# Other slots for kept keys and loads, and whole heads in one load, in a decode kernel over two caches

## The chip, the cores and the metric

The kernel runs on one core of one Trainium2 chip. The core has TensorE (PE, with its weight loads as PEld), VectorE (DVE), ScalarE (ACT), GpSimd (POOL) and SyncE (SP), which here issues every load, and 16 DMA engines that move the data. The metric is device time in microseconds, the median of the runs shown. Before the change it is 1115.87 us over three runs (1115.45 to 1117.47).

## The reference

Eight sequences of one token each (448 numbers) go through attention A, a mixing MLP B, then A and B again with the same weights and the same caches:

```python
x = A_x
x = x + _A_ref(_layernorm(x, axis=-1), A_k_cache, A_v_cache, A_wq, A_wo)
x = x + _B_ref(_layernorm(x, axis=-1), B_w1, B_w2, B_w3, B_w4)
x = x + _A_ref(_layernorm(x, axis=-1), A_k_cache, A_v_cache, A_wq, A_wo)
x = x + _B_ref(_layernorm(x, axis=-1), B_w1, B_w2, B_w3, B_w4)

def _A_ref(x, k_cache, v_cache, wq, wo):        # Hq, Dh = 16, 256; caches (8, 8, 4096, 256), bf16
    q = (x @ wq).reshape(B, Sq, Hq, Dh).transpose(0, 2, 1, 3)
    k = jnp.repeat(k_cache, 2, axis=1)
    v = jnp.repeat(v_cache, 2, axis=1)
    p = softmax(einsum("bhqd,bhkd->bhqk", q, k) * Dh ** -0.5)
    o = jnp.einsum("bhqk,bhkd->bhqd", p, v)
    return o.transpose(0, 2, 1, 3).reshape(B, Sq, Hq * Dh) @ wo
```

With one token, the shifts inside B leave zeros of its first part, so B comes down to `x + h2` with two layer norms and `w3`, `w4`. The key and value caches have 134 MB each; each of them is wanted twice.

## The kernel before

**Units and parts.** A unit is one key/value head of one sequence in one of the two attention passes: `(p, b, g)`, with pass p 1 or 2, sequence b, head g. The keys of a head are 2 MB, and so are the values. They are handled in four parts of 512 KB. A part lies in one slot: 4 KB on each of 128 partitions. The slab holds 31 slots of `UNIT` = 2048 bf16 elements a partition, side by side. In HBM partition p owns 16 KB of a head in one piece (32 rows of 256 numbers), of which part s is the s-th 4 KB.

**Keys.** A key part is loaded raw, transposed by DVE into another slot (L560, two instructions a part, in `transposes`), and the raw slot becomes free. PE multiplies the transposed part with the queries (L651, 16 matmuls, in `k_part`). For heads 2 to 7 the transposed keys stay in their slots from pass 1 to pass 2. Heads 0 and 1 are `loose`: their keys are loaded and transposed again for pass 2. Two parts of head 4 (`parked`) are kept in PSUM banks instead, and ScalarE copies them back into a slot when pass 2 comes near (L518).

**Values.** A value part is read by PE straight from its slot (L628, 16 matmuls, in `v_part`) and loaded again in pass 2. In all there are 320 key parts and 512 value parts.

**Order.** The order of units is written out: per sequence pass 1 of its heads, then two units of other sequences (`lone`) that lie beside the dense layers of the sequence (a generator, `mid_steps`), then pass 2. The unit that ends a pass 1 is in `ends`; `fence` holds the unit with which pass 2 of a sequence begins, because its queries must be done. Each unit has four steps q; at each step the key part of the unit and value parts of an earlier one are multiplied. After the key parts come the maximum over the scores (DVE L666, PE L674, DVE L684), the exponential (ACT L687), the way into rows (PE L700 and L710, ACT L718), the sum (DVE L725, POOL L729), and at the end the scaling of the output (ACT L597).

**Loads.** `loads` is a list in a fixed order, made from the step at which a part is due. `pump` is called wherever a slot comes free, takes loads off the list as long as more than `RESERVE` = 1 slot is free, and issues each on SP (L534). The first loads of weights are spliced in (L543). `free` is the list of slots; `under_way` counts parts that are issued and not yet used up. Stretches between a fence and the next end are `calm`; loads that fall due there are in `wide`, and those some units from its borders in `firm`. If a load of an even part has its neighbour near it in the list and in `wide`, both are loaded in one go into an even slot and the next one. If no such two are free, and `ENOUGH` = 7 parts are under way and the neighbour is in `firm`, `pump` returns and waits; else the part goes alone.

The program is written straight into each engine's queue: an instruction waits in its own queue until the slots that it reads and writes are ready, and what stands behind it waits too. Which slot is taken therefore decides on whom a load, a transpose or a copy waits.

Of the kernel before, what the change touches and what calls it, by code (L numbers as in the profile page):

```python
# [17 lines left out]
RESERVE = 1  # L18
# [4 lines left out]
LEAD = 1  # L23
LAG = 6
ENOUGH = 7
PAIR_VIEW = 12
SETTLE = 3
BEFORE = 1
# [3 lines left out]
def kernel(  # L32
# [333 lines left out]
    loose = heads[: G - KEEP]  # L366

    second = [2, 3, 6, 7, 4, 5]
    parked = {(second[-1], 4 - PARKED + i): i for i in range(PARKED)}
# [3 lines left out]
    lone = {b: [(1, b + 2, g) for g in loose] for b in range(4)}  # L373
    lone.update({4: [(1, 6, 0)], 5: [(1, 6, 1)], 6: [(1, 7, 1)], 7: [(2, 5, 1)]})
    units = []
# [29 lines left out]
    t = 0  # L405
    while t < n_units:
# [5 lines left out]
        n = 1  # L412
# [3 lines left out]
        for j in range(parts_):  # L416
            m = n // parts_ + (j < n % parts_)
# [26 lines left out]
    for t in order:  # L444
        for s in range(4):
            i = late_v.get((t, s), 4 * t + s + LAG)
            if t in ends or units[t + 1 : t + 2] == [GAP]:
                i = 4 * t + (6, 6, 7, 7)[s]
            elif t + 1 == n_units:
                i = 4 * t + (5, 5, 6, 7)[s]  # L450
# [3 lines left out]
    loads = []  # L454
    wide = set()
    calm = [any(f < t for f in [-1] + list(fence) if not any(f < e < t for e in ends)) for t in range(n_units + 2)]
    firm = set()
    at_ease = [all(calm[max(t - SETTLE, 0) : t + BEFORE]) for t in range(n_units + 1)]
    k = 0
    for i in range(4 * n_units + 8):  # L460
        n = len(loads)
# [8 lines left out]
        t, q = divmod(i + 2, 4)  # L470
# [3 lines left out]
    free = list(range(N_SLOTS))  # L474
    raw_of, v_of, kt_of = {}, {}, {}
    under_way = [0]

    def take():

        lone = [x for x in free if x ^ 1 not in free]  # L480
        x = min(lone or free)
        free.remove(x)
        return x

    def take_two():

        both = [x for x in free if x % 2 == 0 and x + 1 in free]
        if both:
            free.remove(both[0])
            free.remove(both[0] + 1)  # L490
        return both[:1]

    extra = []
    for c in range(3):
# [13 lines left out]
    def pump():  # L508
        while loads and len(free) > RESERVE:
            kind, t, i = loads[-1]  # L510
            _, b, g = units[t]
            if kind == "p":
                loads.pop()
                x = take()
                dst = slots[x].rearrange("p (e q c x) -> p q c e x", e=4, q=2, c=4)
                for j in range(2):
                    src = park[parked[g, i]][j][:].bitcast(BF16)
                    nc.scalar.copy(dst[:, j], src.rearrange("p (c e x) -> p c e x", c=4, e=4))  # L518
                kt_of[(1, b, g), i] = x
                continue  # L520
            cache, of = (A_k_cache, raw_of) if kind == "k" else (A_v_cache, v_of)
            n, two = 1, (kind, t, i + 1)
            if i % 2 == 0 and two in wide and two in loads[-PAIR_VIEW:]:
                x = take_two() if len(free) > RESERVE + 1 else []
                if x:
                    n, x = 2, x[0]
                    loads.remove(two)
                elif under_way[0] >= ENOUGH and two in firm:
                    return
            loads.pop()  # L530
            if n == 1:
                x = take()
            src = cache[b, g].rearrange("(p s e) d -> p s (e d)", s=4, e=8)
            nc.sync.dma_start(  # L534
                slab[:, UNIT * x : UNIT * (x + n)].rearrange("p (s d) -> p s d", s=n),
                src[:, i : i + n],
            )
            for m in range(n):
                of[t, i + m] = x + m
            under_way[0] += n  # L540
            n_loads[0] += n
            if n_loads[0] >= 8 and extra:
                nc.sync.dma_start(*extra.pop(0))  # L543
# [3 lines left out]
    def transposes(i):  # L547


        while len(parts) - len(todo) < by[i]:  # L550
            t, s = todo[-1]
            if 4 * t + s > i and ((t, s) not in raw_of or not free):
                return
            todo.pop()
            raw = raw_of.pop((t, s))
            kt = kt_of[units[t], s] = take()
            src = slots[raw].bitcast(FP32).rearrange("p (q c e i) -> p q c e i", q=2, c=4, e=4)
            dst = slots[kt].bitcast(FP32).rearrange("p (e q c r) -> p q c e r", e=4, q=2, c=4)
            for q in range(2):
                nc.vector.transpose(dst[:, q], src[:, q])  # L560
            _, b, g = units[t]
            if (g, s) in parked:
                for q in range(2):
                    dst = park[parked[g, s]][q][:].rearrange("p (c e r) -> p c e r", c=4, e=4)
                    nc.vector.transpose(dst, src[:, q])
            free.append(raw)
            under_way[0] -= 1
            pump()
# [49 lines left out]
    def v_part(t, s):  # L618
        if s == 0:
            at = PO + 4 * (nth[t] % n_po)  # L620
            pos[t] = pyb[:, at : at + 4].rearrange("p (k h) -> p k h", h=2)
            if nth[t] == n_po // 2:
                nc.vector.memset(pyb[:, PO : PO + 4 * (len(order) - n_po)], 0.0)
        v = v_of.pop((t, s))
        vv = slots[v].rearrange("p (c d) -> p c d", d=Dh)
        for c in range(8):
            for k in range(2):
                nc.tensor.matmul(  # L628
                    pos[t][:, k, :],
                    vv[:, c, 128 * k : 128 * k + 128],  # L630
                    pts[t][:, 8 * s + c, :],
                    start=(t == 0 and s == 0 and c == 0 and k == 0),
                    stop=True,
                    skip_group_check=True,
                )
        free.append(v)
        under_way[0] -= 1
        pump()

    def k_part(t, s):  # L640
        u = units[t]
        p, b, g = u
        if s == 0:
            assert t not in runs or t in ready
            scs[t] = scb[t % 2][:, 0:64].rearrange("p (c b h) -> p c b h", b=4, h=2)
        key = (u if fresh(u, s) else (1, b, g)), s
        ktv = slots[kt_of[key]].rearrange("p (e c m x) -> p e c m x", e=4, c=2, x=2)
        for c in range(2):
            for db in range(4):
                for x in range(2):  # L650
                    nc.tensor.matmul(  # L651
                        scs[t][:, 2 * s + c, :, :],
                        ktv[:, db, c, :, x],
                        Qblk[run_of[t][0]][:, run_of[t][1], db, x, :, :],
                        start=(db == 0 and x == 0),
                        stop=(db == 3 and x == 1),
                    )
        if p == 2 or g in loose or (g, s) in parked:
            free.append(kt_of.pop(key))
            pump()  # L660
# [129 lines left out]
    for t in range(n_units + 1):  # L790
        cur = t < n_units
        for q in range(4):
            i = 4 * t + q
            if cur:
                if t in fence and q == 0:
                    flush()
                    while (fence[t], 1) not in q_done:
                        next(dense[0])
                        flush()
                    flush()  # L800
                    make_blocks(t)
                late = q == 0 and t and not beside[t]
                if beside[t]:
                    transposes(i)
                flush()
                if not late and not beside[t]:
                    transposes(i)
                if units[t]:
                    k_part(t, q)
# [4 lines left out]
            if cur and late:  # L814
                transposes(i)
# [130 lines left out]
```

## Time and profile before

| | |
|---|---|
| median of three runs | 1115.87 us |
| the profiled execution | 1116.44 us |
| its span, first to last instruction | 1114.6 us |
| moved by DMA | 449.77 MB, mean 404 GB/s |
| PE, PEld busy | 686.8 us, 640.3 us |
| DVE, ACT, POOL busy | 550.7 us, 307.2 us, 104.4 us |
| loads of keys | 126 of 512 KB, 97 of 1024 KB |
| loads of values | 252 of 512 KB, 130 of 1024 KB |
| DVE transposes (L560) | 640, mean 687 ns |
| granted TensorE clock | 1.00 |

The page's slices cut the span into 40 equal parts; the figure for DMA is the share of time in which the 16 DMA engines were busy, in tenths. A row of the waits says which engine and line waited, for whom, how many microseconds in all, how often, and the longest. In a row of the windows stand the stretch, its length, busy time and instructions of PE, PEld, DVE, ACT and POOL, the clock, the DMA share and GB/s. In the timeline stand start, duration, engine, line, operation, operands, count, and in brackets the idle time before it with what ended it; rows of SPq are issues of loads. An engine that waits costs nothing as long as another is the bottleneck.

### The profile page before, as it was taken

What the parts mean: (1) busy time and instruction counts of PE and PEld (TensorE: products, weight loads), DVE (VectorE), ACT (ScalarE), POOL (GpSimd) and SP (SyncE); (2) the same over time, 40 slices, a digit from 0 to 9 for tenths busy, and PEclk for the clock granted to TensorE, in tenths of its full rate; (3) what the DMA queues carried; (4) which work ended last, traced back from release to release, by engine and by line L of the source; (5) the groups of instructions that cost most, each with busy time, mean ns of one, the idle gap of its engine ahead of it and who ended that gap; (6) DMA issues with size and microseconds to landing.
All of it is one profiled execution on the core that took longest, in us unless ns stands there. A gap on an engine that the chain in (4) does not pass through costs nothing.

```text
span 1114.6 us, 46349 instructions
## 1 busy us (share of the span) xinstructions
PE 686.8 (62%) x20737; PEld 640.3 (57%) x20737; DVE 550.7 (49%) x1305; ACT 307.2 (28%) x1360; POOL 104.4 (9%) x156
## 2 busy tenths in 40 slices
PE   3345675666756566565756667565757566655765
PEld 2334564665646566565656557555756566655765
DVE  4347554644446445554555535553447435554332
ACT  1112124321233212422233212422143212422231
POOL 0001001110011100110011000110011000100001
DMA  9999999999999999999999999999999999999992
GB/s 364 393 417 425 401 417 423 424 418 395 417 423 424 402 401 419 422 424 390 414 420 424 400 410 416 421 423 412 395 419 425 407 411 397 422 422 405 384 413 101
DMA packets 94503, 449.77 MB, mean 404 GB/s; under 512 B 9936, under 2 KB 15968, under 8 KB 64864
## 3 DMA queue, kind: packets, MB, share of 16 engines
q1 hardware_dynamic: 94304, 446.81, 98.4%
q8 instruction: 162, 2.65, 0.8%
q14 instruction: 37, 0.30, 0.1%
HBM read 446.77 MB, written 0.01 MB: 401 GB/s over the span
## 4 chain that ended last, share of the span: by engine, by line
DMA 39%; PE 15%; ACT 6%; issue 5%; DVE 5%; POOL 0%; SPq 0%; DVEq 0%; ACTq 0%; POOLq 0%
DMA slab<-in_A_v_cache_dram 31%; DMA slab<-in_A_k_cache_dram 8%; PE bank L628 5%; PE bank L651 3%; DVE slab L560 3%; ACT pt L718 2%; PE bank L137 2%; ACT slab L518 1%; ACT pe L687 1%; DVE small L684 1%; PE bank L674 1%; PE bank L710 1%; ACT pt_far L718 1%; PE bank L700 1%; PE bank L313 1%
## 5 line engine op out<-in xcount | busy, mean ns | idle before, releaser
L560 DVE STREAM_TRANSPOSE slab<-slab 128x512 f32<-128x512 f32 x640 | 414.7, 687 | 217.6 <-DMA slab<-in_A_k_cache_dram 173.2
L628 PEld LDWEIGHTS <-slab 128*128 128x128 bf16 x8192 | 273.3, 106 | 288.6 <-DMA slab<-in_A_v_cache_dram 223.7
L628 PE MATMUL bank<-pt,slab 128*128 128x2 bf16 x7168 | 261.0, 166 | 235.4 <-DMA slab<-in_A_v_cache_dram 163.6
L651 PE MATMUL bank<-Qblk,slab 128*128 128x8 bf16 x8192 | 297.0, 168 | 77.0 <-DVE slab L560 39.3
L651 PEld LDWEIGHTS <-slab 128*128 128x128 bf16 x8192 | 267.6, 105 | 88.1 <-DVE slab L560 46.4
L687 ACT ACTIVATE pe<-bank,small 128x32 bf16<-128x32 f32 x256 | 61.7, 297 | 407.6 <-DVE small L684 407.5
L729 POOL TENSOR_TENSOR small<-small 128x2 f32<-128x2 f32 x112 | 78.4, 700 | 774.1 <-DVE small L725 774.1
L718 ACT CAST pt<-bank 32x64 bf16<-32x64 f32 x448 | 91.1, 203 | 108.2 <-PE bank L710 104.2
L684 DVE TENSOR_REDUCE small<-bank 128x2 f32<-128x256 f32 x128 | 54.1, 422 | 104.9 <-PE bank L674 104.6
L725 DVE TENSOR_REDUCE small<-bank 128x2 f32<-128x64 f32 x128 | 27.2, 212 | 118.8 <-ACT pt L718 102.6
L166 ACT CAST Qblk<-bank 32x32 bf16<-32x32 f32 (+1 forms) x272 | 48.5, 178 | 109.4 <-PE bank L160 107.0
L674 PE MATMUL bank<-rows,small 128*128 128x128 bf16 x256 | 48.5, 293 | 10.9 <-DVE small L666 10.9
L666 DVE TENSOR_REDUCE small<-bank 128x2 bf16<-128x64 f32 x128 | 26.4, 206 | 55.4 <-PE bank L651 55.2
L628 PE MATMUL bank<-pt_far,slab 128*128 128x2 bf16 x1024 | 36.8, 166 | 26.2 <-DMA slab<-in_A_v_cache_dram 24.6
L710 PE MATMUL bank<-pe,rows 128*128 128x64 bf16 x512 | 51.0, 240 | 1.1 <-issue 1.1
L710 PEld LDWEIGHTS <-rows 128*128 128x128 bf16 x512 | 33.6, 123 | 28.2 <-issue 27.6
L700 PE MATMUL bank<-pe,small 128*128 128x64 bf16 x128 | 27.2, 212 | 31.8 <-ACT pe L687 29.9
L182 PEld LDWEIGHTS <-wo_sb 128*128 128x128 bf16 x1152 | 35.5, 104 | 9.9 <-issue 8.8
L182 PE MATMUL bank<-OT,wo_sb 128*128 128x1 bf16 x1024 | 33.3, 165 | 7.0 <-ACT OT L597 4.5
L137 PEld LDWEIGHTS <-wq_sb 128*128 128x128 bf16 x864 | 30.6, 106 | 12.0 <-issue 7.4
L518 ACT COPY slab<-park 128x1024 bf16<-128x1024 bf16 x32 | 30.1, 1028 | 8.8 <-DVE slab L560 8.7
L137 PE MATMUL bank<-small,wq_sb 128*128 128x1 bf16 x768 | 28.1, 165 | 6.0 <-issue 6.0
(113 smaller groups left out, 384.1 us busy)
## 6 DMA issues: line engine op xcount, KB each, us to landing
slab<-in_A_v_cache_dram SPq DMA_DIRECT2D x130, 1024.0 KB, 13.0
slab<-in_A_v_cache_dram SPq DMA_DIRECT2D x252, 512.0 KB, 8.1
slab<-in_A_k_cache_dram SPq DMA_DIRECT2D x97, 1024.0 KB, 13.7
slab<-in_A_k_cache_dram SPq DMA_DIRECT2D x126, 512.0 KB, 8.9
wo_sb<-in_A_wo_dram SPq DMA_DIRECT2D x4, 896.0 KB, 11.7
wq_sb<-in_A_wq_dram SPq DMA_DIRECT2D x3, 1024.0 KB, 6.9
w_sb<-in_B_w_dram SPq DMA_DIRECT2D x1, 1568.0 KB, 12.4
w_sb<-in_B_w_dram SPq DMA_DIRECT2D x3, 448.0 KB, 16.7
```

Source lines behind the costliest of these rows:

```text
L137: nc.tensor.matmul(pv[:, i, j, :], cols(big[:, c, :], m + i * half), rows[:, c, :], start=(i == 0 and j == 0 and c == 0), stop=True, skip_ ...
L166: nc.scalar.copy(dst, src)
L182: nc.tensor.matmul(y[:, c, :], chunk(wo_sb[:, k, :], c), o[:, k, :], start=False, stop=True, skip_group_check=True,)
L560: nc.vector.transpose(dst[:, q], src[:, q])
L628: nc.tensor.matmul(pos[t][:, k, :], vv[:, c, 128 * k : 128 * k + 128], pts[t][:, 8 * s + c, :], start=(t == 0 and s == 0 and c == 0 and k ...
L651: nc.tensor.matmul(scs[t][:, 2 * s + c, :, :], ktv[:, db, c, :, x], Qblk[run_of[t][0]][:, run_of[t][1], db, x, :, :], start=(db == 0 and x ...
L674: nc.tensor.matmul(mzs[t][:, 128 * h : 128 * h + 128], pm[:, h : h + 1].to_broadcast([128, 128]), ident, start=True, stop=True,)
L684: nc.vector.tensor_reduce(nm, mx, AX.X, ALU.max, negate=True)
L687: nc.scalar.activation(pe[:].rearrange("p c b h -> p h (c b)")[:, h], scs[t].rearrange("p c b h -> p h (c b)")[:, h], ACT.Exp, bias=nm[:, ...
L710: nc.tensor.matmul(pp[:, c], sel, pe[:], start=True, stop=True)
L718: nc.scalar.copy(pts[t][sl].rearrange("p (k c) h -> p k c h", c=4), pp[sl, :, :, pb, :].rearrange("p c k h -> p k c h"),)
L729: nc.gpsimd.tensor_tensor(out=rz_of[t], in0=zs, in1=mone, op=ALU.pow)
```

## The change

Slots are picked in another way, and a third size of load is added.

- A transposed key part that is kept until pass 2 goes into the lowest free slot. Everything else (single loads, transposed parts of loose or parked heads, copies from the parked banks) goes to the upper end of the shortest run of adjacent free slots, searched from the top. Before, every single slot was the lowest of those whose neighbour in the pair was taken, or else the lowest.
- Loads of more than one part take the shortest run of free slots that is long enough, at any position, from its upper end. Before, two parts needed an even slot and the next.
- A load that begins with part 0 is first tried as a whole head: four parts, 2 MB, 16 KB in one piece for each partition, if all are in `wide` and near in the list. If no four adjacent slots are free and at least `PLENTY` = 8 parts are under way, and the last of the four is in `firm`, `pump` waits; else two are tried as before, else one.

The instructions of PE, DVE and POOL and their order stay the same. In ScalarE's queue the copies from the parked banks stand a few instructions later in five of the eight sequences. SP has fewer loads.

```diff
@@ -23,6 +23,7 @@
 ENOUGH = 7
+PLENTY = 8
 PAIR_VIEW = 12
@@ -475,20 +476,28 @@
-    def take():
-
-        lone = [x for x in free if x ^ 1 not in free]
-        x = min(lone or free)
-        free.remove(x)
+    def take(low=False):
+
+        x = min(free) if low else take_run(1)
+        if low:
+            free.remove(x)
         return x
 
-    def take_two():
-
-        both = [x for x in free if x % 2 == 0 and x + 1 in free]
-        if both:
-            free.remove(both[0])
-            free.remove(both[0] + 1)
-        return both[:1]
+    def take_run(n):
+
+        x, best = max(free) + 1, None
+        while x > 0:
+            x -= 1
+            hi = x
+            while x >= 0 and x in free:
+                x -= 1
+            if hi - x >= n and (best is None or hi - x < best[0]):
+                best = hi - x, hi - n + 1
+        if best is None:
+            return None
+        for m in range(n):
+            free.remove(best[1] + m)
+        return best[1]
@@ -519,17 +528,20 @@
             cache, of = (A_k_cache, raw_of) if kind == "k" else (A_v_cache, v_of)
-            n, two = 1, (kind, t, i + 1)
-            if i % 2 == 0 and two in wide and two in loads[-PAIR_VIEW:]:
-                x = take_two() if len(free) > RESERVE + 1 else []
-                if x:
-                    n, x = 2, x[0]
-                    loads.remove(two)
-                elif under_way[0] >= ENOUGH and two in firm:
-                    return
+            x = None
+            for n, may, must, enough in ((4, wide, firm, PLENTY), (2, wide, firm, ENOUGH)):
+                more = [(kind, t, i + m) for m in range(1, n)]
+                if i % n == 0 and all(y in may and y in loads[-PAIR_VIEW:] for y in more):
+                    x = take_run(n) if len(free) >= RESERVE + n else None
+                    if x is not None:
+                        for y in more:
+                            loads.remove(y)
+                        break
+                    if under_way[0] >= enough and more[-1] in must:
+                        return
             loads.pop()
-            if n == 1:
-                x = take()
+            if x is None:
+                n, x = 1, take()
@@ -553,7 +565,7 @@
-            kt = kt_of[units[t], s] = take()
+            kt = kt_of[units[t], s] = take(units[t][2] not in loose and (units[t][2], s) not in parked)
```

## The prediction

> **What bounds the kernel now.** I read the slices and queues of the page first, then windows of one kind of load, then the waits, then the end.
>
> ```profile
> DMA  9999999999999999999999999999999999999992
> GB/s 364 393 417 425 401 417 423 424 418 395 417 423 424 402 401 419 422 424 390 414 420 424 400 410 416 421 423 412 395 419 425 407 411 397 422 422 405 384 413 101
> ...
> q1 hardware_dynamic: 94304, 446.81, 98.4%
> ...
> slab<-in_A_v_cache_dram SPq DMA_DIRECT2D x130, 1024.0 KB, 13.0
> slab<-in_A_v_cache_dram SPq DMA_DIRECT2D x252, 512.0 KB, 8.1
> slab<-in_A_k_cache_dram SPq DMA_DIRECT2D x97, 1024.0 KB, 13.7
> slab<-in_A_k_cache_dram SPq DMA_DIRECT2D x126, 512.0 KB, 8.9
> ```
>
> The DMA engines are full until the last slice (98.4%), while PE is busy 62% and DVE 49%. So the time is the sum of the packet times on an engine, the idle time between them, and a tail. Loads are 252 + 126 = 378 single parts (4 KB runs) and 130 + 97 = 227 pairs (8 KB runs).
>
> ```profile
> 180.00:240.00 60.00, 36.92 (x1135) 34.73 (x1135) 33.50 (x71) 21.12 (x88) 6.00 (x9) 1.00 1.01 424
> 260.00:300.00 40.00, 28.75 (x869) 27.06 (x866) 20.60 (x59) 8.47 (x41) 3.35 (x5) 1.00 1.02 412
> 380.00:400.00 20.00, 12.06 (x347) 11.42 (x347) 7.74 (x22) 3.73 (x19) 1.40 (x2) 1.00 0.99 370
> 920.00:940.00 20.00, 14.05 (x456) 13.57 (x453) 11.01 (x23) 5.43 (x26) 1.95 (x3) 1.00 1.01 386
> 1040.00:1060.00 20.00, 15.62 (x498) 15.01 (x496) 7.39 (x19) 7.88 (x34) 2.65 (x4) 1.00 0.99 372
> ```
>
> The last two columns are DMA share and GB/s. All pairs: 424 GB/s, 8192 x 16 / 424 = 309 ns a packet. All singles: 412 GB/s, 159 ns. The trace's packet records have these as medians. Two singles cost 318 ns, one pair 309: a run costs 9 ns beyond its bytes. The other three windows lie where the dense layers run: slots come free too slowly, and 26 to 42 GB/s are missing, 1.3 to 2.1 us in each 20 us.
>
> ```profile
> PE bank L628 <- DMA slab<-in_A_v_cache_dram: 188.2, 157, 3.8
> DVE slab L560 <- DMA slab<-in_A_k_cache_dram: 173.2, 84, 8.9
> DVE slab L560 <- PE bank L628: 38.0, 22, 4.6
> ```
>
> PE and DVE wait for data all along, so time saved in the stream counts. From 1040 us on, the waits of the window have 1.2 us on K and none on V: the last 75 us are a compute chain and gain nothing.
>
> **What is removed: runs.** The changed program's list of SP's DMAs has 346 singles, 97 pairs and 73 loads of four, 516 in place of 605. A load of any kind is 128 runs, 8 for each of the 16 engines. Each load less saves 8 x 9 ns, and the 4-byte record that ends a load on each engine, 9 ns in the packet records: 81 ns. 89 loads are 7.2 us; 5 of them are after 1040 us: **-6.8 us**. This takes 2 x 309 - 9 = 609 ns for a run of 16 KB, which no K or V row shows. Ends: if it is moved as two of 8 KB, only 16 loads' worth of runs is saved: 16 x 72 ns + 0.8 = 2.0 us. The only packets of 16 KB are the 162 of the instruction queue, 0.8% of 16 x 1114.6 us, 0.88 us each; at that price 584 such runs an engine cost 584 x 0.26 = 150 us more. I take 609, since 4 to 8 KB shows the pure 9 ns and the instruction packets share full engines with the data.
>
> 89 issues less on SP, 0.33 us each, cost and save nothing: SP waits for slots most of the time.
>
> **What is added: larger units of landing.** For each load of the changed list I timed the release of its slots by the trace of before (end of the matmuls or transposes that last read them) and the moment when the queue would be dry by the bytes moved so far.
>
> (a) The first part of a load of four lands with the last, up to 1 MB / 424 GB/s = 2.5 us later than in a pair. At some 20 uses it would come after the use of before, by 2.0 to 3.4 us (keys of units 43, 61, 79, 96, 113, values of 23, 41, 59, 77, 94, 111, 128), mostly one key and one value head a batch, shortly before the dense layers. Behind the waiting value matmul in PE's queue stand the key matmuls and slot releases; behind a waiting transpose stand DVE's three reductions of a unit. The queue holds 6 to 10 parts (7 to 12 us) there, which hides most. Ends 0 and 7 x 4 = 28 us; I take **+2**.
>
> (b) With 8 or more parts under way a load now waits until four adjacent slots are free, though up to 12 scattered ones are. Lead of the issue over the dry queue falls to 1.6 us at unit 25's keys (203.6 us) and 0.8 us at unit 57's values (467.1 us). In the program of before it goes under 2.6 us only at 637, 884, 920 and 1044, two of them in the low windows above; so I count what is missing to 3 us: 1.4 + 2.2 = **+3.6**. Two further places (0.0 us at 324.9, 1.2 at 456.7) I count at nothing: the transpose that frees the slot waited there for PE to read values out of its destination (the 38.0 us row), and its new destination is free 6 to 7 us earlier. Without that cover they cost 4.8 more. Ends 0 and 8.4.
>
> (c) The eight fences, where pass 2 of a batch begins. Right after a key part's matmuls free a slot, one load and one transpose take a slot, and two are free: an old one and the one just freed. Before, the lowest went to the load; now the load searches from the top and takes the old one, and the transpose gets the one PE is still to read. So DVE waits for PE:
>
> ```profile
> 920.38 4.03 DVE L560 STREAM_TRANSPOSE slab<-slab 128x512 f32<-128x512 f32 x6 [0.30 <-DMA slab<-in_A_k_cache_dram]
> ...
> 925.18 0.22 PE L651 MATMUL bank<-Qblk,slab 128*128 128x8 bf16 x3 [1.84 <-issue]
> ...
> 927.53 0.23 DVE L666 TENSOR_REDUCE small<-bank 128x2 bf16<-128x64 f32 x1 [3.12 <-PE bank L651]
> 927.82 0.40 PE L674 MATMUL bank<-rows,small 128*128 128x128 bf16 x2
> ```
>
> The three parts transposed from 920.38 start when these matmuls end, 925.4: +5.0 us. By the same two rows the other fences give +3.1, 0.6, 0.9, 1.4, 2.9, 4.6, and 2.6 at 1044. Behind them in DVE's queue stands the maximum (L666), which PE's L674 waits for: 925.4 + 4.0 = 929.4 for 927.53, 1.9 us late; 1.8 at 802, 2.6 at 158, under 1 elsewhere. One value load goes out some 3 us earlier, the next waits for the transposes: the smallest lead falls from about 2.8 to 1.6 us at 805 and 928, from 3.8 to 2.4 at 682. Missing to 3 us, beyond before: 1.3 + 1.1 + 0.6 = 3.0, and 1.5 for the late maxima, which leads of 4 to 6 us behind them mostly cover: **+4.5**. Ends 0 and 21 (all eight waits on the path).
>
> (d) In the tail nothing covers the fence at 1044: its second part ends 1050.1 for a maximum at 1049.33, +0.8. And ScalarE's four copies out of the parked banks (L518), 3.76 us at 1058.7, move behind the exponential at 1062.28, in front of the casts (L718) at 1063.32: casts at 1066.4, done 1067.2, for value matmuls that started 1066.69, +0.5 to +0.7. **+1.5** (0 to 2.6 + 3.8). The values of the last four heads come in fours, but land 2 us or more before their use (1095 for 1099.5): nothing.
>
> In four earlier batches the copies move behind the output scaling, once behind the query copies too. At 316 us PE stood 6.61 us for that scaling; a stall of PE goes, but the DMA was full meanwhile: nothing.
>
> **Sum.** -6.8 + 2 + 3.6 + 4.5 + 1.5 = +4.8 us. The profiled execution took 1116.44 us (span 1114.6 and 1.8 around it), so 1121.2; it stands 0.57 above the median of the runs, 1115.87, and so **1120.7 us**.
>
> **Rivals.** *Faster:* slots come free earlier than I count. Keys in low slots end DVE's 38.0 us of waits for PE's value reads in the wide stretches, so (a) and (b) have more lead. It decides when the lead at 467 us is 3 us: without (a) and (b) 1115.1, and with half of (c) covered 1112.9. For it: at 324.9 and 456.7 it plainly happens. Against: at 467 the release is a key matmul, not a transpose. *Cancelling:* losses of 5 to 9 us, 1114 to 1118, about 1116. *Runs of 16 KB are cut in two:* the gain is 2.0, not 6.8: 1125.5. Against it stands only that 4 to 8 KB was clean.
>
> *Code behind larger packets:* an instruction packet that waits for one data packet more in front waits 609 - 309 = 0.3 us longer. In the tail PE stalls for "issue" up to 2.3 us at six fetches, 1.8 us in all; elsewhere PE has waits for V to spare: 1122.5. Against: the instruction packets took 0.93 us beside 4 KB and 8 KB packets alike. The Trainium skill, "DMA: Bandwidth & Descriptors", section "Queues, rings and completion order", has each engine take turns between queue rows packet by packet, finishing a packet before it switches; by that rule this rival would hold, and the trace from 4 to 8 KB does not show it.
>
> **How the numbers follow.** Forecast 0.46, code 0.03, cut runs 0.07: slower 0.56. Cancelling: same 0.17. Faster rival 0.27. About 0.2%, 2.2 us, can be told from no change. The range goes from the whole gain with no loss, 1109, to the forecast with losses (a) to (d) near double, 1129; the forecast's own is 1118.2 to 1129. Leads and landings are laid on the old timeline, so each of (a) to (d) can be off by its half.
>
> **What would show it.** Right: SP's list with 2048 KB loads, windows between fences at about 430 GB/s (16384 x 16 / 609), DVE L560 waiting for PE L651 some 20 us in total, DVE's wait for L628 well under 38, PE's longest wait for V nearer 5 than 3.8 us, windows at the fences of 800 and 920 below before. Wrong: q1's share stays at 98.4% with no lower windows, or windows of fours at 424 or far below.

## The result: 1142.75 us, 2.5% slower

The changed kernel takes 1142.75 us (median of five runs, 1141.55 to 1147.34) against 1115.87 us for the kernel before on the same chip (1115.04 to 1118.45): a ratio of 1.0247, interval 1.0234 to 1.0260. The forecast was 1120.7 us, with a range up to 1129. The side was right and the size was wrong: the loss is 26.9 us where 4.8 was forecast.

The profiled execution after the change took 1147.34 us, with a span of 1145.3. First the slices, the first queue and the loads of the page of the changed kernel (line 534 of before is now 546, and all later lines move by 12 too):

```profile
DMA  7999999999999999999999999999999999999992
GB/s 284 410 414 370 358 403 414 405 399 403 417 425 424 375 413 416 424 405 387 415 421 427 387 407 406 401 421 379 405 406 430 379 382 393 409 393 408 384 398 111
...
q1 hardware_dynamic: 81488, 446.81, 96.5%
...
slab<-in_A_v_cache_dram SPq DMA_DIRECT2D x232, 512.0 KB, 8.0
slab<-in_A_v_cache_dram SPq DMA_DIRECT2D x43, 2048.0 KB, 12.9
slab<-in_A_k_cache_dram SPq DMA_DIRECT2D x30, 2048.0 KB, 14.3
```

The bytes are the same, in 14% fewer packets, and yet the rates in the slices are mostly lower. The share of the queue falls from 98.4 to 96.5%: the engines now have gaps, beginning with the first slice (284 for 364). Next, windows of the changed kernel; the last two columns are DMA share and GB/s:

```profile
0.00:20.00 20.00, 4.39 (x124) 3.85 (x124) 3.69 (x34) 4.01 (x10) 1.54 (x9) 1.00 0.63 226
100.00:140.00 40.00, 21.22 (x558) 18.38 (x556) 26.93 (x53) 10.20 (x50) 3.48 (x5) 1.00 0.92 342
...
340.00:360.00 20.00, 11.43 (x344) 10.95 (x341) 12.02 (x26) 6.44 (x31) 2.79 (x4) 1.00 1.01 428
380.00:400.00 20.00, 14.40 (x465) 13.82 (x463) 9.96 (x22) 5.83 (x28) 2.09 (x3) 1.00 0.95 373
860.00:880.00 20.00, 12.34 (x365) 11.59 (x362) 11.05 (x24) 6.58 (x33) 2.79 (x4) 1.00 1.02 431
900.00:920.00 20.00, 11.41 (x370) 10.97 (x369) 8.01 (x17) 4.74 (x23) 2.10 (x3) 1.00 0.91 345
```

The same windows of the kernel before, but for 380 us, which the prediction shows:

```profile
0.00:20.00 20.00, 5.65 (x164) 5.05 (x164) 7.63 (x41) 4.01 (x10) 1.55 (x9) 1.00 0.88 341
340.00:360.00 20.00, 13.09 (x423) 12.12 (x421) 13.00 (x27) 5.87 (x28) 2.10 (x3) 1.00 1.01 423
860.00:880.00 20.00, 13.00 (x413) 12.22 (x413) 10.32 (x22) 5.15 (x26) 1.40 (x2) 1.00 1.01 424
900.00:920.00 20.00, 14.95 (x442) 14.31 (x443) 6.48 (x32) 2.76 (x13) 1.40 (x2) 1.00 1.02 415
100.00:140.00 40.00, 24.05 (x653) 21.26 (x652) 25.41 (x61) 7.55 (x37) 3.49 (x5) 1.00 1.02 408
```

Where the queue is full and mostly fours are moved, at 340 and 860 us, the rate is 428 and 431 GB/s; before it was 423 and 424 in the same windows. So the gain is there. Around it are new holes: the first 20 us (226 GB/s for 341), 100 to 140 us (342 for 408), 900 to 920 us (345 for 415).

The start of each unit's first key matmul in the two traces shows when the time goes. The first unit is 6.4 us late. At unit 12 (155.0 us before, 168.3 after) it is 13.3 us, at unit 36 16.1, at unit 60 18.0, at unit 88 22.3, at unit 124 31.3 us. So some of it goes at the very start, and the rest in steps all along.

For the following comparisons I made one account from the packet records of each profiled execution, as a mean over the 16 DMA engines up to the last byte of keys and values. "Runs" is the number of packets of 4, 8 and 16 KB times 159, 309 and 609 ns. "Long" is what those packets took beyond that. "Idle" is the time in which an engine had no packet. All else (small packets, weights, code, less what overlaps) is 15 to 18 us in each kernel.

| kernel | runs | long | idle | last byte |
|---|---|---|---|---|
| before | 1050.6 | 20.6 | 8.9 | 1095.5 |
| after | 1044.2 | 36.4 | 27.7 | 1125.7 |

The profiled execution after is 4.6 us above the median, so the account has 30.2 us for a loss of 26.9. The runs save 6.4 us. But 18.8 us of idle engines come in, and 15.8 us of long packets. The long ones lie beside the idle time: packets over 1.2 times the usual add up to 20.2 us before and 34.0 after, and of this, what started within stretches of 2 us with over 0.1 us idle, or next to them, rises from 5.7 to 18.9 us. So the new long packets lie where the engines had gaps. That the gaps make them long is argued from this place, and no run tests it.

### The profile page after: what moved, and what is told of

It is laid out like the page before. It is cut to its first block, busy times and chain, and to the rows that moved or that the text cites. A ratio compares the mean times of both kernels' runs of the same rounds, so it can differ in the third digit from the quotient of the medians.

```text
span 1145.3 us, 46175 instructions
## 1 busy us (share of the span) xinstructions
PE 684.6 (60%) x20737; PEld 643.3 (56%) x20737; DVE 547.6 (48%) x1305; ACT 306.0 (27%) x1360; POOL 104.1 (9%) x156
## 3 DMA queue, kind: packets, MB, share of 16 engines
q1 hardware_dynamic: 81488, 446.81, 96.5%
## 4 chain that ended last, share of the span: by engine, by line
DMA 55%; PE 20%; DVE 8%; issue 8%; ACT 7%; SPq 1%; POOL 1%; DVEq 0%; ACTq 0%; POOLq 0%
DMA slab<-in_A_v_cache_dram 27%; DMA slab<-in_A_k_cache_dram 23%; PE bank L640 7%; DVE slab L572 5%; PE bank L663 5%; DMA wo_sb<-in_A_wo_dram 2%; ACT pt L730 2%; PE bank L138 2%; DVE small L696 2%; PE bank L686 2%; ACT pe L699 2%; DMA w_sb<-in_B_w_dram 2%; PE bank L183 1%; PE bank L722 1%; PE bank L712 1%
## 5 line engine op out<-in xcount | busy, mean ns | idle before, releaser
L663 PE MATMUL bank<-Qblk,slab 128*128 128x8 bf16 x8192 | 297.9, 168 | 87.1 <-DVE slab L572 51.0
L663 PEld LDWEIGHTS <-slab 128*128 128x128 bf16 x8192 | 268.5, 105 | 97.7 <-DVE slab L572 56.8
L737 DVE TENSOR_REDUCE small<-bank 128x2 f32<-128x64 f32 x128 | 27.7, 216 | 113.2 <-ACT pt L730 98.7
L722 PEld LDWEIGHTS <-rows 128*128 128x128 bf16 x512 | 33.7, 124 | 34.9 <-issue 34.5
L183 PEld LDWEIGHTS <-wo_sb 128*128 128x128 bf16 x1152 | 35.6, 104 | 20.2 <-DMA wo_sb<-in_A_wo_dram 11.9
L183 PE MATMUL bank<-OT,wo_sb 128*128 128x1 bf16 x1024 | 33.5, 165 | 18.4 <-DMA wo_sb<-in_A_wo_dram 11.9
L686 PEld LDWEIGHTS <-small 128*128 128x128 bf16 x256 | 16.7, 106 | 43.3 <-DVE small L678 42.1
L138 PEld LDWEIGHTS <-wq_sb 128*128 128x128 bf16 x864 | 30.7, 106 | 11.8 <-issue 7.5
## 6 DMA issues: line engine op xcount, KB each, us to landing
wo_sb<-in_A_wo_dram SPq DMA_DIRECT2D x4, 896.0 KB, 20.2
```

The costliest lines, as they stand in the source:

```text
L138: nc.tensor.matmul(pv[:, i, j, :], cols(big[:, c, :], m + i * half), rows[:, c, :], start=(i == 0 and j == 0 and c == 0), stop=True, skip_ ...
L183: nc.tensor.matmul(y[:, c, :], chunk(wo_sb[:, k, :], c), o[:, k, :], start=False, stop=True, skip_group_check=True,)
L663: nc.tensor.matmul(scs[t][:, 2 * s + c, :, :], ktv[:, db, c, :, x], Qblk[run_of[t][0]][:, run_of[t][1], db, x, :, :], start=(db == 0 and x ...
L686: nc.tensor.matmul(mzs[t][:, 128 * h : 128 * h + 128], pm[:, h : h + 1].to_broadcast([128, 128]), ident, start=True, stop=True,)
L722: nc.tensor.matmul(pp[:, c], sel, pe[:], start=True, stop=True)
```

## The experiments

Each ratio below is to the kernel before on the same chip. Its median lay between 1115.66 and 1117.39 us, so kernels that ran on different chips are better compared by their ratios than by their microseconds.

### The start

The setup of the kernel keeps its scratch in `slots[-1]` to `slots[-4]`, the last four slots. The kernel before took slots from the bottom. The changed one takes the first loads from the top, where the scratch is. This is the list of SP's issues in the timeline of the changed kernel (start, duration):

```profile
3.22 0.59 SPq L113 DMA_DIRECT2D wq_tl<-in_A_wq_dram  x1
16.33 0.98 SPq L546 DMA_DIRECT2D slab<-in_A_k_cache_dram  x2
```

In the kernel before the first load of keys is issued at 3.97 us. The waits of SP in the first 60 us of the changed kernel name the holder, a setup matmul that reads the scratch:

```profile
SPq L546 <- PE bank L146: 8.9, 1, 8.9
...
SPq L546 <- DVE slab L791: 3.5, 1, 3.5
```

The first experiment moves the scratch out of the way:

```diff
-    xw = slots[-1]
+    xw = slots[7]
...
-    identb = slots[-4][:, 1024:1152]
+    identb = slots[4][:, 1024:1152]
...
```

The other two, `slots[-2]` and `slots[-3]`, become `slots[6]` and `slots[5]`.

> The changed kernel with the setup's scratch (four slots, 27 to 30) moved to slots 4 to 7, so that the first loads, which now start at the top, no longer wait for the setup. Theory (the loss begins at the start): the first K load goes out at about 4 us in place of 16.3, the window from 0 to 20 us comes back from 226 GB/s to about 340, and the time falls by what is missing there, (341 - 226) x 20 / 424 = 5.4 us, up to the 6.4 us by which the first key matmul is late: 1136 to 1138 for 1142.75. Rival (the start is made up for later, since the later stalls come from slots and not from the data): 1141 to 1143.

Measured: 1136.74 us (1133.91 to 1136.96), ratio to before 1.0178 (1.0158 to 1.0197), within the theory's range. The first load goes out at 3.94 us, the window from 0 to 20 us has 342 GB/s, and 6.0 us are won by the medians, 0.7% by the ratios, whose intervals leave 4 to 11 us. The late start costs about what the stream misses, and nothing shows that it is made up for later. The opposite test puts the scratch of the kernel before in the way of its own first loads:

```diff
-    xw = slots[-1]
+    xw = slots[0]
...
-    identb = slots[-4][:, 1024:1152]
+    identb = slots[3][:, 1024:1152]
...
```

The other two become `slots[1]` and `slots[2]`.

> The kernel before with only its scratch moved into the way of the first loads (slots 0 to 3 in place of 27 to 30), nothing else. Theory (a late start costs what the stream misses, whatever the allocator): the first load goes out at about 16 us, +5 to +7 us, 1121 to 1123. Rival (the kernel before makes up for it later): 1116 to 1118.

Measured: 1119.36 us (1118.36 to 1121.0), ratio 1.0029 (1.0018 to 1.0041), between the two expectations. The size missed because the first load goes out at 6.72 us, not at 16; only the second waits until 16.62 us, and the other two behind it. The four issues are done at 18.40 us, and the window from 0 to 20 us has 272 GB/s. What is missing there, (341 - 272) x 20 / 424 = 3.3 us, is what was measured, 0.29%.

The second suspect was the weights: one weight transfer is issued behind each load, and a load of four is one load.

```diff
-            if n_loads[0] >= 8 and extra:
-                nc.sync.dma_start(*extra.pop(0))
+            for _ in range(max(1, n // 2)):
+                if n_loads[0] >= 8 and extra:
+                    nc.sync.dma_start(*extra.pop(0))
```

> The changed kernel, with two of the ten weight transfers issued behind each load of four in place of one; the scratch stays at the top. Theory (late weights): the first pass's output layer no longer waits 11.9 us for wo, the window from 100 to 140 us comes back from 342 GB/s towards 408, and the time falls by up to (408 - 342) x 40 / 424 = 6 us: 1136 to 1140. Rival (the low windows of the first 170 us come from the late start alone, so the weights are late for the same reason): 1142 to 1144.

> Scratch in slots 4 to 7 and two weight transfers behind each load of four, together. Theory: the drift of 13 us that the changed kernel has by 168 us goes almost whole, 1129 to 1132, and what stays over the kernel before, 13 to 16 us, is the fences and the wait for four adjacent slots, (c) and (b) of the prediction. Rival (the drift of the first 170 us is the fours' own, slots that come free together): no more than the 5 to 6 us of the late start are won, 1136 to 1138.

Measured: 1146.47 us (1142.79 to 1146.63) with the weights alone, ratio 1.0260 (1.0235 to 1.0285), and 1136.23 us (1134.37 to 1141.47) with both, ratio 1.0187 (1.0157 to 1.0216). The first lies above both of its ranges, with an interval that overlaps the changed kernel's; the second is the rival's number. PE's wait of 11.9 us for `wo` is gone in both, and no time with it. This theory falls. The 100 to 140 us window stays low with both edits (366 GB/s), so it does not come from the weights. The rest of the experiments start from the kernel with the scratch in slots 4 to 7, 1136.74 us.

### The loads of four, or the new order of the slots

```diff
-            for n, may, must, enough in ((4, wide, firm, PLENTY), (2, wide, firm, ENOUGH)):
+            for n, may, must, enough in ((2, wide, firm, ENOUGH),):
```

> The changed kernel with the scratch in slots 4 to 7 (1136.74 us) without the entry for loads of four: keys low and loads from the top stay, 122 + 244 singles and 99 + 134 pairs, about as the kernel before has. Theory (the wait for four adjacent slots starves the queue all along): most of the 20.8 us that are left over the kernel before goes, 1118 to 1123, the rest being the fences. Rival (the new order of the slots does it, at the fences above all): 1131 to 1138.

Measured: 1123.1 us (1120.67 to 1124.93), ratio 1.0059 (1.0036 to 1.0082). That is the upper edge of the theory's range. Taking the fours away thus wins 1.2 of the 1.78% that are left. The other 0.6 are not a fixed price of the new order of the slots: two kernels below that take slots by the same rule and load fours, one from 12 parts on, one as two of two, stand at 1.0020 and 1.0018.

```diff
-PLENTY = 8
+PLENTY = 12
```

> The changed kernel with the scratch in slots 4 to 7, and 12 parts under way in place of 8 before a load waits for four adjacent slots: 26 loads of four are left of 73. Theory (the wait starves the queue): at 12 parts the queue is far from dry when it begins, and the time falls at least by the share of fours that go, to 1120 to 1128. Rival (the order of the slots): 1133 to 1138.

Measured: 1118.86 us (1117.96 to 1120.22), ratio 1.0020 (1.0010 to 1.0029), lower than expected, and lower than without fours. With 26 fours in place of 73 nearly the whole loss is gone.

The fours on the old slots (runs of four only at multiples of four, singles chosen as before):

```diff
+        lone = [x for x in free if x ^ 1 not in free]
+        x = min(lone or free)
...
+        for x in range(0, N_SLOTS - n + 1, n):
+            if all(x + m in free for m in range(n)):
```

> The loads of four of the change (37 come about) on the slots of the kernel before: a single or a key part in the lowest slot whose neighbour is taken, pairs and fours in the lowest slots that lie at a multiple of two or four; scratch at the top, out of the way. Theory (waiting for adjacent slots costs, whichever slots): 1124 to 1134. Rival (the loss is the new order's of the slots): 1113 to 1118, with 37 x 2 fewer runs of 9 ns an engine as the gain.

Measured: 1117.13 us (1114.92 to 1119.54), ratio 1.0010 (0.9999 to 1.0021). That fits the rival. But it does not clear the fours, since only 37 of them come about there, and in its account the runs save 3.8 us while long packets take 3.7 more than before. With `PLENTY` = 12 on the old slots:

> Loads of four on the slots of the kernel before, waiting for them from 12 parts under way in place of 8: 18 are left of 37. Theory (waiting at 8 costs what the runs save): a little under 1117.13, 1114 to 1117. Rival (these waits cost nothing there, so that fewer fours mean a smaller gain): 1117 to 1119.

Measured: 1116.57 us (1115.06 to 1119.35), ratio 0.9994 (0.9983 to 1.0005). That is within the theory's range, but the interval tells it neither from the kernel before nor from the one with 8.

### One load of four, or two loads of two

This experiment keeps every slot and every point where `pump` returns to wait for four, and only issues the four as two:

```diff
-            nc.sync.dma_start(
-                slab[:, UNIT * x : UNIT * (x + n)].rearrange("p (s d) -> p s d", s=n),
-                src[:, i : i + n],
-            )
+            h = min(n, 2)
+            for m in range(0, n, h):
+                nc.sync.dma_start(
+                    slab[:, UNIT * (x + m) : UNIT * (x + m + h)].rearrange("p (s d) -> p s d", s=h),
+                    src[:, i + m : i + m + h],
+                )
```

> The changed kernel with the scratch in slots 4 to 7, same slots and same waits, but each load of four issued as two loads of two (8 KB runs). Theory (a run costs 9 ns beyond its bytes, and a load's record 9 ns): the time rises by 73 x 81 ns = 5.9 us, 1142 to 1143 for 1136.74. Rival (the first part of a four lands late, (a) of the prediction, and costs about what the runs save): 1134 to 1138.

Measured: 1119.3 us (1113.72 to 1122.3), ratio 1.0018 (1.0004 to 1.0032), against 1.0178. Both expectations were far off: I had thought that the planner's waiting for four adjacent slots starves the queue, and it hardly does. The two loads of two give up the runs' gain (1049.5 for 1044.2 us in the account) and still win 17.4 us.

Three reasons were left. One issue waits for the last of four slots, with all other loads behind it. The first part lands with the last. Or 16 KB runs have a price that the packet records don't show. Two more experiments keep the pairs and change their order:

```diff
-            for m in range(0, n, h):
+            for m in range(n - h, -1, -h):
```

> As the kernel with each load of four issued as two of two (1119.3 us, same slots), but the second pair of parts is issued ahead of the first. So the first part, which is needed first, now waits for all four slots and lands last, as in a load of four; the runs stay at 8 KB. Theory (one load of four waits for the last of four slots and lands late): most of the 17.4 us come back, 1131 to 1137. Rival (16 KB runs have a price of their own that starves the queue): 1118 to 1122.

```diff
+            x, age = None, {y: k for k, y in enumerate(free)}
...
+            newest = max(range(n), key=lambda m: age[x + m]) // h * h
+            for m in [newest] + [n - h - newest] * (n > 2):
```

> As the kernel with each load of four issued as two of two, but the pair that holds the slot freed last is issued first, so that nothing of a four goes out before all four slots are free; in 51 of the 73 that is the second pair, in 22 the first. Theory 1 (what costs is waiting for the last of four slots, SP standing still meanwhile): 1131 to 1137, as with the second pair first. Theory 2 (what costs is the late landing of the first part): between, 1126 to 1133, since in 22 fours it lands early. Rival (16 KB runs): 1118 to 1122.

Measured: 1136.95 us (1135.03 to 1138.42) with the second pair first, ratio 1.0187 (1.0169 to 1.0205), as the theory had it; 1127.58 us (1127.43 to 1129.07) with the pair freed last first, ratio 1.0109 (1.0091 to 1.0126), in the range of theory 2. The first comes back to the loads of four without a single run of 16 KB, so the third reason falls as the main one. It is not excluded altogether: the loads of four take the same time although their runs save 5.3 us, and what eats these 5.3 us may be that their second pair waits too, or another price of the large runs. The two differ only in the 22 fours whose first pair holds the slot freed last (last in the program's list `free`, which is not always the last by the clock): there the first pair waits as long, but lands ahead of the second. These 22 alone are worth 0.8%, 9 us. So the late first part counts by itself, and the rest, up to 10 us, is waiting for the last slot together with the late first part of the other 51. A kernel that has that waiting alone was not made, so these two are not told apart further.

SP's waits in the traces, for the kernel with fours, with pairs in order, and with the second pair first (total, times, longest):

```profile
SPq L546 <- PE bank L640: 261.2, 174, 11.5
```

```profile
SPq L548 <- PE bank L642: 251.5, 190, 8.5
```

```profile
SPq L548 <- PE bank L642: 280.1, 174, 11.2
```

And for the kernel before, and the fours on the old slots:

```profile
SPq L534 <- PE bank L628: 202.8, 174, 5.0
```

```profile
SPq L538 <- PE bank L632: 281.6, 198, 9.9
```

Among the first three the total changes little. What changes is that SP stands up to 11 us at a stretch for a value part to be read, and all later loads stand behind it. The longest wait alone does not make the loss, though: on the old slots it is 9.9 us, and the kernel loses nothing that shows. The Trainium skill, "DMA: Bandwidth & Descriptors", section "Anatomy of one DMA — SWDGE (gpsimd) path", says in a note that DMA engines never wait on semaphores themselves and that every such wait is done by the issuing sequencer; the rows agree, for SP on its own kind of queue. The account of these kernels:

| kernel | runs | long | idle | last byte |
|---|---|---|---|---|
| fours, scratch moved | 1044.2 | 33.0 | 17.6 | 1111.8 |
| as two of two | 1049.5 | 24.3 | 9.9 | 1099.8 |
| second pair first | 1049.5 | 30.2 | 17.5 | 1113.1 |
| pair freed last first | 1049.5 | 27.3 | 17.3 | 1109.9 |
| `PLENTY` = 12 | 1048.2 | 22.7 | 8.2 | 1095.0 |

Each row is one profiled execution: 1133.91 us with fours and 1122.30 as two of two, so the account shows 12.0 of the 17.4 us between the medians.

How near the queue is to dry can be read from the end of each issue and the bytes that had landed by then. Between 150 and 1060 us, the changed kernel issues its fours with a median of 4.1 parts still in the queue, and 12 of 54 with less than two (some 2.5 us). The pairs of the kernel before have 6.3, and 3 of 184 have less than two. With `PLENTY` = 12 it is 6.7 parts for 15 fours, and none under 4. So the 8 parts "under way" of the planner are about 4 in the queue; the others have landed and wait to be read. The median is not what counts, however: the fours on the old slots find 2.8 parts, fewer still, but only 2 of 23 find less than two, and the idle time is 8.8 us, as before the change. Counted over all loads of more than one part, those that find less than two are 19 in the changed kernel, 15 with the scratch moved, 17 with the second pair first and 9 with the pair freed last first. In the kernels that lose little they are fewer: 6 as two of two, 8 with `PLENTY` = 12, 5 on the old slots, and 3 before. Among these kernels a loss of over 1% comes with 9 or more such loads, and the median does not sort them.

### The fences

```diff
-    def pump():
+    def pump(newest=False):
...
-                n, x = 1, take()
+                n, x = 1, free.pop() if newest else take()
...
             free.append(kt_of.pop(key))
-            pump()
+            pump(beside[t] or t in fence)
```

The flag also takes in the units beside the dense layers (`beside`), which lie just ahead of each fence.

> The changed kernel with the scratch in slots 4 to 7, where the single load that follows a key part's matmuls at a fence takes the slot that these have just freed, so that the transpose gets the older one: 351 of its loads are singles. Theory (the waits of DVE for PE L663, 39.9 us in the changed kernel, cost what the prediction has as (c), near their double): they fall under 10 us in total, and the time by 6 to 10 us, 1127 to 1131. Rival (the load that now waits for PE in their place, or the wait for four slots, costs as much): 1134 to 1138.

Measured: 1137.77 us (1135.59 to 1138.24), ratio 1.0192 (1.0176 to 1.0207): nothing won, as the rival had it. The edit also shifts what is merged a little; the profile has 348 singles, 100 pairs and 71 fours. The waits of DVE for slots, in the kernel with the scratch moved first, then with this edit:

```profile
DVE slab L572 <- DMA slab<-in_A_k_cache_dram: 169.3, 61, 11.2
...
DVE slab L572 <- PE bank L663: 41.0, 13, 4.9
...
DVE slab L572 <- PE bank L640: 20.2, 10, 4.0
```

```profile
DVE slab L572 <- DMA slab<-in_A_k_cache_dram: 199.0, 72, 11.1
...
DVE slab L572 <- PE bank L640: 13.5, 7, 4.1
```

The wait for PE's key matmuls falls from 41.0 to 1.0 us, as meant, and DVE waits 30 us more for keys instead. The same edit on the kernel without fours, and with `PLENTY` = 12:

> The kernel without loads of four (new slots, scratch in slots 4 to 7, 1123.1 us), where at a fence the load that follows a key part's matmuls takes the slot that these have just freed. Theory (c): the 36.9 us that DVE waits there for PE L663 go, and with them the 6 us over the kernel before, 1116 to 1119. Rival (as at 8 parts under way, the wait moves to the load, which now waits for PE): 1121 to 1125.

> New slots, scratch in slots 4 to 7, waiting for four adjacent slots from 12 parts under way, and the just freed slot for the load at the fences. Theory (the queue stays full and the fences are free): 1112 to 1116. Rival (the fences' order costs nothing on the path): 1117 to 1120, as without it (1118.86).

Measured: 1119.71 us (1117.52 to 1122.27), ratio 1.0024 (1.0013 to 1.0035), for 1.0059 without the edit; and 1118.28 us (1116.32 to 1120.1), ratio 1.0012 (1.0001 to 1.0022), for 1.0020. The first lies between its two ranges, the second in the rival's. Without fours the fences' order thus costs 0.35%, some 4 us, and the two intervals just do not overlap. DVE's wait for PE L663 falls from 36.9 to 1.8 us there. With `PLENTY` = 12 it is about 1 us, which the intervals don't separate.

### The weights once more, and a faster kernel

With the queue not starved, the late weights could still show:

> Loads of four on the old slots, waiting from 12 parts under way (1116.57 us), with two weight transfers behind each load of four. Theory (the weights are late by the fours, and where the queue is not starved it shows): PE's wait for wo of 11.9 us goes and with it 1 to 3 us, 1113.5 to 1115.5, under the kernel before. Rival (that wait is made up for, as where the queue was starved): 1116 to 1118.

> The same edit of the weights on the new slots, with the fences' order mended, waiting from 12 parts under way (1118.28 us). Theory: 1115 to 1117. Rival: 1118 to 1119.

Measured: 1117.66 us (1114.73 to 1119.64), ratio 0.9999 (0.9989 to 1.0009), and 1117.53 us (1114.19 to 1122.27), ratio 1.0001 (0.9989 to 1.0014). The wait for `wo` is gone again. For the first it is the rival's number; the second lies between the two ranges, 0.1% under the same kernel without the edit, with overlapping intervals. So the late weights cost nothing that shows. No kernel here is shown to beat the one before.

## Why the prediction was wrong

**The bound and the gain were right.** The time follows the stream: the last byte lands 30.2 us later, and the span is 30.7 us longer. The median packet of 16 KB took 611 ns for 609 forecast, windows of fours run at 428 to 431 GB/s, and the runs save 6.4 us for 6.8. So the rival of cut runs falls. The Trainium skill, "DMA: Bandwidth & Descriptors", section "Rules for kernel authors", wants at least 1 MiB for each DMA for the highest bandwidth. Pairs meet that already, single parts of 512 KB do not. The rates here agree with it (412 GB/s for single parts, 424 for pairs, 428 to 431 for fours), but the rule is about bandwidth alone: the time of this kernel went the other way.

**Code behind larger packets** finds no support either. The median instruction packet took 0.935 us before and 0.938 after, and 0.94 us beside 16 KB packets (the 0.88 us of the prediction came from a rounded share). PE's waits for "issue" ahead of key and value matmuls are 45.9 us before, 49.3 after, and 56.4 with the second pair first, where no K or V run is larger than 8 KB.

**The start was not costed at all.** The prediction followed each load of the new list from the trace of before, but not the first ones, whose slots change from the bottom to the top, where the setup's scratch lies. This is some 6 us. "89 issues less ... cost and save nothing" held for the weights too, though they were not named: they do come later, and it costs nothing.

**(a) and (b) were sized at +5.6; the fours cost 17.4 us net of the 5.3 us that their runs save, some 23 us.** This is the step that failed. The prediction had both mechanisms, and said that the queue "holds 6 to 10 parts there, which hides most", and counted only what was missing to 3 us at two places. In the changed kernel the fours find 4.1 parts in the queue, not 6 to 10, and 12 of 54 find less than two. Six find less than 1 us of work: the values of units 25, 43, 79, 92 and 126 and the keys of unit 132. None of these is a place that the prediction counted in (b). At its own two places, the keys of unit 25 and the values of unit 57, the queue has 0.7 us (forecast 1.6) and 2.2 us (forecast 0.8). The loads and landings were laid on the timeline of before, where pairs kept the queue full. That the loss feeds itself, since a four that goes out late is read late and the next four waits for its slots, is likely but only argued. Of (b), the holding in the planner costs little: it stays in the fours issued as two of two, 1.0018. The price lies in the issue, which waits for the last of four slots, and in the landing; of these, 9 us of late landing are shown by themselves. The upper ends given, 28 and 8.4 us, did hold it; the values chosen lay near the lower ones. Nothing was set aside for the long packets, 15.8 us beside 18.8 us of new idle time.

**(c) was found, mis-sized, and then not on the path.** DVE's waits for PE's key matmuls came, 39.9 us for about 21 forecast. Here are DVE's rows of the changed kernel, and PE's row for values:

```profile
DVE slab L572 <- DMA slab<-in_A_k_cache_dram: 173.9, 58, 16.9
...
DVE slab L572 <- PE bank L663: 39.9, 13, 5.1
...
DVE slab L572 <- PE bank L640: 20.9, 10, 3.8
```

```profile
PE bank L640 <- DMA slab<-in_A_v_cache_dram: 156.7, 118, 5.9
```

With the fours starving the queue, taking these waits away wins nothing; without fours it wins about 4 us, near the 4.5 forecast. DVE's wait for PE's value reads fell from 38.0 to 20.9 us, as forecast, though not by the low slots alone: with the same rule for slots and no fours it is 34.5 us. And PE's longest wait for values rose past the 5 us forecast to 5.9.

**(d)** was not tested by itself. From the last byte to the end of the span it is 19.1 us before and 19.6 after, so 0.5 us of the forecast 1.5 shows in that stretch. With 6.0 for the start, 23 for the fours and 6.4 saved by the runs, 4 to 5 us of the 26.9 are left for the fences, the tail and the new order of the slots together, against the 6.0 forecast for (c) and (d). That these agree is in part luck, since (c) wins nothing where the fours are loaded.

**The rivals.** The faster one rested on slots that come free earlier. Some do (38.0 to 20.9 us above), but its condition, a lead of 3 us at the narrow place near 467 us, did not come about: there it was 2.2 us, and elsewhere fours went out with under 1 us. The cancelling rival, with losses of 5 to 9 us, falls with the size of the loss.

## What to carry to other kernels

A larger load is paid for not by its bytes but by its slowest slot and its first part: before merging loads, ask when the last of its slots is released and when its first part is wanted, and keep the queue deep enough for both. Count what is in the queue and not what is issued and unread, and look for the loads that find it nearly dry, not at the usual depth. Splitting a merged load in two with all else kept is a cheap test of this, and swapping the halves tells waiting and landing together from the size of the runs. When an allocator changes its direction, look at what else lies in those buffers at the start.

## What the runs showed of the hardware

A run of 16 KB costs 611 ns, one of 8 KB 309 and one of 4 KB 159, so joining two runs saves 9 ns from 4 to 8 KB and 7 ns from 8 to 16 KB. Not expected was that the packets beside a gap in the stream are long as well: 18.8 us of idle engines came with 15.8 us of long packets, single ones of 16 KB up to 2.45 us. That the dry queue causes them is only argued, from where they lie.
